# Input loads in thirds, and routed rows written one at a time over a longer stretch, in an attention-and-experts kernel

## The chip, the cores and the metric

The kernel runs on one core of a Trainium2 chip, as one program. The metric is the device time of one execution in microseconds; several executions are timed and their median counts. TensorE (PE in the rows, its weight loads PEld), VectorE (DVE), ScalarE (ACT), GpSimd (POOL) and SyncE (SP) each run their own instructions in program order, and wait for each other and for DMA transfers by semaphores. Plain transfers are issued on SP, indirect ones (rows addressed by a list of indices) on GpSimd.

## What is computed

Two steps in float32, cut from the reference. First a linear recurrence per batch (4) and head (8) over 768 steps with a head size of 48:

```python
for t in range(S):
    cur = einsum('bhd,bhe->bhde', u[None] * kt, vt)
    y[:, :, t] = einsum('bhd,bhde->bhe', rt, state + cur)
    state = wt[:, :, :, None] * state + einsum('bhd,bhe->bhde', kt, vt)
```

Then y, as 3072 rows x of 384, goes through a mixture of 8 experts with one expert per row:

```python
logits = x @ w_gate + modality_bias[modality_id]
e_idx = argmax(logits)
gate_w = probs[arange(N), e_idx]                 # softmax of logits
for e in range(E):
    h = maximum(x[e_idx == e] @ w1[e], 0.0)      # 384 -> 1024
    out[e_idx == e] = gate_w * (h @ w2[e])       # 1024 -> 384
```

## The kernel before

**Attention part.** The 3072 rows are cut into 24 units of 128 rows. The loop `for i in range(-2, NU)` calls `att_iter(i)`, which works on three units at a time: unit i+2 in its first stage (VectorE's scan and the spread of r and k), unit i+1 in its second (TensorE's scores, the mask A of L403, the state), unit i in its last (the products into pY, L445), while GpSimd prepares unit i+3 (the decays L278, G of L283, L295). The order of the work on each engine is the order in which the code is written; there is no scheduler.

A unit's inputs are r, k and w, each a third of 512 columns of one buffer `in0` to `in3` (768 KB for 128 partitions), and v, in a buffer of its own (4 of them). `load(n)` (L106) issues the transfer of unit n on SP, in one piece or cut by columns. SP works in order: a transfer whose buffer is still in use holds those behind it.

**Routing.** A unit's finished rows go into `xp` (L464), and once the rows of a part are routed (`route_a`, `route_b`), each unit's 128 rows of 386 columns are written to their places in the DRAM tile `xs` by one indirect transfer: `scatter(n)`, L692, on GpSimd, 128 row indices in a column of `posT`. `route_b` fills `posT` for all units of a part with one reduction (L574). Part 0 is units 0 to 9, part 1 units 10 to 23. `hook_b(c)` appends the units of part c to the list `pend`, and `drain(n)` scatters the next n of them. `pad_rows(e)` (L684, on SP) writes 128 rows of zeros behind expert e's rows. Rows of part 0 lie in memory that the weights of the first down-projection (`wh[1]`, `wl[1]`) use later.

**Experts part.** Seven blocks q0 to q6 of up to 512 routed rows. For each: `blk_load` reads the block's rows from `xs` into `xl` (L718, SP; block 0's and block 1's during attention, at the iterations in `LOAD`), `blk_t` transposes them (TensorE L733, ScalarE xh L743, VectorE xo L745), eight `blk_up` (the ups: 9 matmuls each, L756, into PSUM tile pS0 or pS1 in turn; then hh on ScalarE L760 and the remainder hl on VectorE L761), up to four `blk_down` (the downs, one for each 128 rows: 24 matmuls, L777), each with `blk_out` (ot on ScalarE L800, an indirect write of 128 output rows on GpSimd, L801). The weights come by `blk_raw` (L267, SP) and are split into a rounded part wh (ScalarE, L272) and a remainder wl (L273, GpSimd or VectorE) by `w_split`. A table, `at(q, "u" or "d", step, ...)`, says what else is written after each up ("u", steps 0 to 7) or after each two of a down's eight slices ("d", four steps for each down); `run` carries it out. By it the 14 units of part 1 are scattered two at a time after q0's "d" steps 2 to 8.

Transfers that read rows of `xs` wait for the scatters that were written ahead of them in the program to land, and scatters behind such a read wait until it has landed; scatters and pads are declared independent of each other.

Of the kernel before, what the change touches and what calls it, by code (L numbers as in the profile page):

```python
# [14 lines left out]
ALU = mybir.AluOpType  # L15
# [47 lines left out]
NEAR = 6  # L63
DRAIN = {**{SCATTER + 2 + n: 1 for n in range(NEAR)}, NU - 3: PART[0] - NEAR}
EARLY = 6
NPW = 3
LOAD = (SCATTER + 1 + NEAR, NU - 2)


@with_exitstack  # L70
def kernel(ctx: ExitStack, tc: tile.TileContext, rkw, vt, wf, cst, mid, wg, bias, w1, w2, out):
# [238 lines left out]
    def ok(n):  # L310
        return 0 <= n < NU
# [244 lines left out]
    def route_b(c):  # L556
# [13 lines left out]
        for j in range(n):  # L570
            m = n + (c == 0 and j < NEAR)
            add(pR[:, (j + 1) * E:(m + 1) * E], onesb, oh[:, j:j + 1].to_broadcast([P, m - j, E]), stop=j == n - 1)
        po, rk = posT[:, units(c)], rcol(C_RK, n, E)
        nc.vector.tensor_reduce(out=po, in_=rk, axis=AX.X, op=ALU.min)  # L574
        sm = wt(c, "sm", [P, NMOST, 1], 1)[:, 0:n]
        nc.vector.tensor_reduce(out=sm, in_=ex[:, 0:n], axis=AX.X, op=ALU.add)
        nc.vector.reciprocal(out=T["xp", c][:, :, DM:DM + 1], in_=sm)

    MAGIC = 12582912.0
# [143 lines left out]
    def blk_t(q):  # L723
        xl, w = X["xl", q], width(q)
        xh, xo = (bp["m"].tile([P, KC, BW], F32R, tag=t, name=f"{t}{q}", bufs=1) for t in ("xh", "xo"))
        pk, pu, nj = pt(f"x{q}_0", "pK", (P, 2, 512)), pt(f"x{q}_2", "pU"), w // P
        halves, m = [(0, KC - 1, (pk[:, 0], pk[:, 1])), (KC - 1, KC, (pu, pt(f"x{q}_3", "pX")))], w % P
        for c0, c1, pp in halves:
# [129 lines left out]
    def drain(n):  # L858
        for _ in range(n):
            if pend:  # L860
                scatter(pend.pop(0))

# [4 lines left out]
    for i in range(-2, NU):  # L867
# [13 lines left out]
        if i >= -1 and ok(i + 3):  # L881
            loadv(i + 3)
        if ok(i + 5):
            load(i + 5)
        if i == 0:
            early()

        drain(DRAIN.get(i, 0))
# [42 lines left out]
    at(q0, "d", 0, part(route_x, 1))  # L931
    at(q0, "d", 1, part(hook_b, 1))
    for g in range(2, 4 * FC // 2):
        at(q0, "d", g, part(drain, 2))
        if g < 6:
            at(q0, "d", g, part(w_split, 0, g - 2))
        if 5 <= g < 8:
            at(q0, "d", g, part(more_table, 1, 2 - g // 7))
# [5 lines left out]
    for e in range(E):  # L944
        at(q1, "u", e // 2, part(pad_rows, e))
    at(q1, "u", 4, part(blk_raw, seq[2], 0), part(blk_load, seq[2]))
    for k, q in enumerate(seq[1:1 + NG // 2]):
# [13 lines left out]
    for n, q in enumerate(seq):  # L961
# [5 lines left out]
        for g in range(FC):  # L967
            blk_up(q, g)
            run(q, "u", g)
        if nxt is not None:  # L970
            blk_t(nxt)
        for j in range(nj):
            for g in range(FC // 2):
                blk_down(q, (2 * g, 2 * g + 1), (j,))
# [199 lines left out]
```

## Time and profile before

| | us |
|---|---|
| timed runs | 362.39, 364.48, 364.92 |
| median of the three | 364.48 |
| profiled execution | 362.38 |
| span of its trace | 360.6 |
| TensorE busy | 338.0 (94%) |
| VectorE busy | 224.4 (62%) |
| ScalarE busy | 206.2 (57%) |
| GpSimd busy | 155.1 (43%) |
| mean granted TensorE clock | 0.972 of full |

The profiled execution took 362.38 us, of which 360.6 lie in the span. A busy share is an average over both parts, so the table alone says little: it is read by stretches (windows), in which one engine's busy time stands beside the clock that TensorE was granted (1.00 is its upper level, 2.4 GHz, and 0.50 its lower, 1.2 GHz) and the share of the time in which the DMA engines moved data. In a timeline each line is one instruction, or several alike in a row (x and their count): its start in the span, its duration, and in brackets how long the engine had been idle and what ended that. "issue" means that the profile shows nothing that the engine waited for, "remote" that what it waited for is not among the recorded events.

### The profile page before, as it was taken

How to read it: one execution, taken by the hardware profiler on the slowest of the kernel's cores; microseconds unless marked ns; L12 is line 12 of the kernel's file. 1: busy time of each engine (PE TensorE's matmuls, PEld its weight loads, DVE VectorE, ACT ScalarE, POOL GpSimd, SP SyncE). 2: the span in 40 equal slices, each digit the busy share in tenths (PEclk: the TensorE clock that was granted, in tenths of full speed). 3: DMA queues.
4: the chain of work that ended last, by engine and by line, in shares of the span. 5: the costliest groups of instructions: out<-in, count | busy, mean ns of one | idle time of the engine just before them, and what ended most of it. 6: DMA issues, size and time to landing. Idle time of an engine off the chain costs nothing.

```text
span 360.6 us, 10329 instructions
## 1 busy us (share of the span) xinstructions
PE 338.0 (94%) x4064; PEld 306.5 (85%) x4064; DVE 224.4 (62%) x478; ACT 206.2 (57%) x524; POOL 155.1 (43%) x194
## 2 busy tenths in 40 slices
PE   8899999999989799997499999999999999999993
PEld 3688899989889687896278999999999988999973
DVE  6999999999997244880057936946526525814500
ACT  2576687878789373620046835956956934614320
POOL 5889999999982860077410220120120120121013
PEclk9999999999999789999589999999999999999998
DMA  7977887778864320036640430160260442210001
GB/s 229 399 242 227 287 291 267 248 258 259 284 225 135 97 82 0 3 139 249 217 164 3 148 137 2 29 236 0 51 236 2 153 158 89 88 58 29 1 25 56
DMA packets 18910, 52.30 MB, mean 145 GB/s; under 512 B 2405, under 2 KB 10405, under 8 KB 18852
## 3 DMA queue, kind: packets, MB, share of 16 engines
q1 hardware_dynamic: 15748, 42.08, 35.3%
q0 software_dynamic: 3104, 9.47, 7.0%
q8 instruction: 34, 0.56, 0.7%
q14 instruction: 24, 0.20, 0.2%
HBM read 55.43 MB, written 11.88 MB: 187 GB/s over the span
## 4 chain that ended last, share of the span: by engine, by line
issue 52%; PE 11%; POOL 9%; POOLq 2%; DMA 1%; ACT 0%; DVE 0%; ACTq 0%
POOL out L801 6%; PE pY L445 3%; POOL xs L692 2%; PE pS L401 2%; PE pY L434 1%; POOLq L984 1%; PE pR_x L317 1%; PE pR_x L494 1%; PE pU L419 1%; DMA xs<-xp,posT 1%; PE pS_u L756 1%; POOL wl L273 1%; POOLq L801 0%; POOLq L964 0%; POOL xp L549 0%
## 5 line engine op out<-in xcount | busy, mean ns | idle before, releaser
L801 POOL DMA_INDIRECT out<-ot,xl x25 | 26.0, 1039 | 157.8 <-ACT ot L800 156.6
L761 DVE SCALAR_TENSOR_TENSOR hl<-pS_u,hh 128x512 fp32r<-128x512 f32 (+2 forms) x56 | 34.6, 618 | 88.3 <-ACT hh L760 74.8
L756 PE MATMUL pS_u<-xh,wh 128*128 128x512 f32 (+2 forms) x168 | 63.1, 375 | 3.0 <-issue 3.0
L756 PE MATMUL pS_u<-xh,wl 128*128 128x512 f32 (+2 forms) x168 | 62.4, 371 | 2.4 <-issue 2.4
L760 ACT ACTIVATE hh<-pS_u 128x512 fp32r<-128x512 f32 (+2 forms) x56 | 30.3, 541 | 51.7 <-PE pS_u L756 50.3
L273 DVE TENSOR_TENSOR wl<-raw,wh 128x768 fp32r<-128x768 f32 x52 | 48.2, 954 | 3.1 <-ACT wh L272 2.6
L756 PE MATMUL pS_u<-xo,wh 128*128 128x512 f32 (+2 forms) x168 | 44.2, 369 | 1.7 <-issue 1.7
L272 ACT CAST wh<-raw 128x768 fp32r<-128x768 f32 (+1 forms) x60 | 45.1, 800 | 0.0
L756 PEld LDWEIGHTS pS_u<-xh,wh 128*128 128x128 f32 x168 | 32.1, 191 | 9.0 <-issue 5.9
L692 POOL DMA_INDIRECT xs<-xp,posT x24 | 24.9, 1040 | 32.3 <-issue 25.0
L777 PE MATMUL pY_d<-wh,hh 128*128 128x384 f32 x112 | 38.5, 344 | 0.0
L777 PE MATMUL pY_d<-wl,hh 128*128 128x384 f32 x112 | 37.6, 336 | 0.0
L777 PE MATMUL pY_d<-wh,hl 128*128 128x384 f32 x112 | 37.6, 336 | 0.0
L756 PEld LDWEIGHTS pS_u<-xh,wl 128*128 128x128 f32 x168 | 32.1, 191 | 5.8 <-issue 2.8
L756 PEld LDWEIGHTS pS_u<-xo,wh 128*128 128x128 f32 x168 | 31.3, 190 | 5.0 <-issue 1.6
L331 DVE TENSOR_TENSOR_SCAN pX_s<-pw,pX_s 128x268 f32<-128x268 f32 x48 | 34.1, 710 | 1.1 <-POOL pw L278 0.8
L283 POOL TENSOR_TENSOR G<-in 128x512 f32<-128x512 f32 x24 | 31.0, 1293 | 4.6 <-DMA in<-rkw 4.6
L445 PE MATMUL pY<-v,A 128*64 128x48 f32 x768 | 29.0, 225 | 2.9 <-issue 2.9
L342 ACT ACTIVATE dV<-v,dT 128x48 f32<-128x48 f32 x120 | 29.7, 325 | 0.1
L445 PEld LDWEIGHTS pY<-v,A 128*64 128x64 f32 x768 | 26.3, 141 | 4.0 <-issue 3.7
L403 DVE TENSOR_TENSOR A<-pS,cs 128x1024 f32<-128x1024 f32 x24 | 29.2, 1217 | 0.6 <-PE pS L401 0.6
L401 PE MATMUL pS<-R,K 64*128 64x128 f32 x384 | 26.9, 280 | 2.0 <-DVE A L403 1.2
(327 smaller groups left out, 679.9 us busy)
## 6 DMA issues: line engine op xcount, KB each, us to landing
raw<-w SPq DMA_DIRECT2D x24, 768.0 KB
in<-rkw SPq DMA_DIRECT2D x22, 768.0 KB
v<-vt SPq DMA_DIRECT2D x24, 192.0 KB
wg<-wf SPq DMA_DIRECT2D x8, 576.0 KB
raw<-w SPq DMA_DIRECT2D x8, 384.0 KB
xl<-xs SPq DMA_DIRECT2D x3, 772.0 KB
xl<-xs SPq DMA_DIRECT2D x4, 579.0 KB
xs<-zt SPq DMA_DIRECT2D x8, 193.0 KB
```

Of the source, the lines that this page charges most:

```text
L272: nc.scalar.copy(out=wh[k][:, sl], in_=raw[k][:, sl])
L273: (eng or (nc.vector, nc.gpsimd)[k]).tensor_tensor(out=wl[k][:, sl], in0=raw[k][:, sl], in1=wh[k][:, sl].bitcast(F32), op=ALU.subtract)
L283: nc.gpsimd.tensor_tensor(out=G, in0=t[:, 0:512], in1=t[:, 512:1024], op=ALU.mult)
L331: nc.vector.tensor_tensor_scan(out=BE[:, ::step], data0=pp[:, ::step], data1=d1[:, ::step], initial=0.0, op0=ALU.mult, op1=ALU.max)
L401: nc.tensor.matmul(out=pS[:, hh, p], lhsT=K[q, p], rhs=R[q, p], start=True, stop=True)
L445: nc.tensor.matmul(out=pY[q:q + 64, h * D:(h + 1) * D], lhsT=A[:, hh, p, q:q + 64], rhs=v[:, h * D:(h + 1) * D], start=(first(z) and h == ...
L692: rows_apart("xs", nc.gpsimd.indirect_dma_start(out=xs[:, :], out_offset=bass.IndirectOffsetOnAxis(ap=posT[:, n:n + 1], axis=0), in_=T["xb ...
L756: nc.tensor.matmul(out=pp, lhsT=wsrc[0][:, g, c * P:(c + 1) * P], rhs=xsrc[:, c, 0:w], start=(n == 0), stop=(n == 3 * KC - 1))
L760: nc.scalar.activation(out=hh, in_=pp, func=AF.Relu)
L761: nc.vector.scalar_tensor_tensor(out=hl, in0=pp, scalar=0.0, in1=hh.bitcast(F32), op0=ALU.max, op1=ALU.subtract)
L777: nc.tensor.matmul(out=X["y", q, j][0:r1 - r0], lhsT=hsrc[:, r0:r1], rhs=wsrc[1][:, f], start=(f == 0 and n == 0), stop=(f == FC - 1 and n ...
L801: ins = nc.gpsimd.indirect_dma_start(out=out[:, :], out_offset=bass.IndirectOffsetOnAxis(ap=xl[0:m, j, DM + 1:DM + 2].bitcast(I32), axis=0 ...
```

## The change

Four things change; the computation stays the same.

1. **Loads.** Before, iteration i ended with unit i+5's whole load. Now unit 3 is loaded whole at i = -2, and from then on iteration i loads k and r of unit i+6, and w of unit i+6 (up to i = 0) and of unit i+7 (from i = 0 on), each as a transfer of 256 KB into its third of the buffer.
2. **Part-0 scatters.** Before, units 0 to 5 went out one at each iteration 15 to 20 and units 6 to 9 together at 21. Now units 0 to 7 go out one at each of 15 to 22 and units 8 and 9 at 23. Block 0's rows are still read at iteration 20, block 1's at 23 instead of 22.
3. **Part-1 scatters.** Before, two after each of seven "d" steps of block 0. Now one each after its "d" steps 2, 3, 4, 8 and 12, one after each of block 1's eight ups, and one after block 1's "d" step 0. Each is preceded by a reduction of its own unit's column of `posT` (`place`); part 0's is done at once as before.
4. **Block 2's rows.** They are read after block 1's "d" step 1 instead of after its up 4, and transposed ahead of block 1's last down instead of ahead of its first, with another PSUM tile.

```diff
--- before.py
+++ after.py
@@ -61,10 +61,10 @@
 NEARLY = 3
 SCATTER = PART[0] + 3
 NEAR = 6
-DRAIN = {**{SCATTER + 2 + n: 1 for n in range(NEAR)}, NU - 3: PART[0] - NEAR}
+DRAIN = {**{SCATTER + 2 + n: 1 for n in range(PART[0] - 2)}, NU - 1: 2}
 EARLY = 6
 NPW = 3
-LOAD = (SCATTER + 1 + NEAR, NU - 2)
+LOAD = (SCATTER + 1 + NEAR, NU - 1)
 
 
 @with_exitstack
@@ -570,11 +570,15 @@
         for j in range(n):
             m = n + (c == 0 and j < NEAR)
             add(pR[:, (j + 1) * E:(m + 1) * E], onesb, oh[:, j:j + 1].to_broadcast([P, m - j, E]), stop=j == n - 1)
-        po, rk = posT[:, units(c)], rcol(C_RK, n, E)
-        nc.vector.tensor_reduce(out=po, in_=rk, axis=AX.X, op=ALU.min)
+        if c == 0:
+            place(0, n)
         sm = wt(c, "sm", [P, NMOST, 1], 1)[:, 0:n]
         nc.vector.tensor_reduce(out=sm, in_=ex[:, 0:n], axis=AX.X, op=ALU.add)
         nc.vector.reciprocal(out=T["xp", c][:, :, DM:DM + 1], in_=sm)
+
+    def place(n, k):
+        c = int(n >= PART[0])
+        nc.vector.tensor_reduce(out=posT[:, n:n + k], in_=rcol(C_RK + (n - FROM[c]) * E, k, E), axis=AX.X, op=ALU.min)
 
     MAGIC = 12582912.0
 
@@ -724,7 +728,7 @@
         xl, w = X["xl", q], width(q)
         xh, xo = (bp["m"].tile([P, KC, BW], F32R, tag=t, name=f"{t}{q}", bufs=1) for t in ("xh", "xo"))
         pk, pu, nj = pt(f"x{q}_0", "pK", (P, 2, 512)), pt(f"x{q}_2", "pU"), w // P
-        halves, m = [(0, KC - 1, (pk[:, 0], pk[:, 1])), (KC - 1, KC, (pu, pt(f"x{q}_3", "pX")))], w % P
+        halves, m = [(0, KC - 1, (pk[:, 0], pk[:, 1])), (KC - 1, KC, (pu, pt(f"x{q}_3", "pS1" if q == WB else "pX")))], w % P
         for c0, c1, pp in halves:
             for c in range(c0, c1):
                 for j in range(nj):
@@ -858,7 +862,10 @@
     def drain(n):
         for _ in range(n):
             if pend:
-                scatter(pend.pop(0))
+                n = pend.pop(0)
+                if n >= PART[0]:
+                    place(n, 1)
+                scatter(n)
 
     def hook_b(c):
         route_b(c)
@@ -880,11 +887,18 @@
         att_iter(i)
         if i >= -1 and ok(i + 3):
             loadv(i + 3)
-        if ok(i + 5):
-            load(i + 5)
+        if i == -2:
+            load(3)
         if i == 0:
             early()
-
+        if ok(i + 6):
+            load(i + 6, ((512, 1024),))
+            load(i + 6, ((0, 512),))
+        for n in range(NEARLY):
+            if i == n - 2:
+                load(n + NIN, ((1024, LIN),))
+        if i >= NEARLY - 3 and ok(i + 3 + NIN):
+            load(i + 3 + NIN, ((1024, LIN),))
         drain(DRAIN.get(i, 0))
         if i in LOAD:
             blk_load(LOAD.index(i))
@@ -930,8 +944,10 @@
     at(q0, "u", FC - 1, part(next, ra1), part(next, ra1), part(blk_raw, q1, 1))
     at(q0, "d", 0, part(route_x, 1))
     at(q0, "d", 1, part(hook_b, 1))
+    for q, ph, steps in ((q0, "d", (2, 3, 4, 8, 12)), (q1, "u", range(FC)), (q1, "d", (0,))):
+        for g in steps:
+            at(q, ph, g, part(drain, 1))
     for g in range(2, 4 * FC // 2):
-        at(q0, "d", g, part(drain, 2))
         if g < 6:
             at(q0, "d", g, part(w_split, 0, g - 2))
         if 5 <= g < 8:
@@ -943,7 +959,8 @@
             at(q, "u", FC - 1, part(blk_raw, nq, 1))
     for e in range(E):
         at(q1, "u", e // 2, part(pad_rows, e))
-    at(q1, "u", 4, part(blk_raw, seq[2], 0), part(blk_load, seq[2]))
+    at(q1, "u", 4, part(blk_raw, seq[2], 0))
+    at(q1, "d", 1, part(blk_load, seq[2]))
     for k, q in enumerate(seq[1:1 + NG // 2]):
         for n, ph, step in ((2 * k, "u", 2), (2 * k + 1, "u", 6)):
             at(q, ph, step, part(guard_load, n))
@@ -967,9 +984,11 @@
         for g in range(FC):
             blk_up(q, g)
             run(q, "u", g)
-        if nxt is not None:
+        if nxt is not None and q != q1:
             blk_t(nxt)
         for j in range(nj):
+            if q == q1 and j == nj - 1:
+                blk_t(nxt)
             for g in range(FC // 2):
                 blk_down(q, (2 * g, 2 * g + 1), (j,))
                 if nxt is not None and q != q0 and j == 0:
```

GpSimd's rows at the end of the attention part and in blocks 0 and 1, before. `xp` are the routed rows (the first five scatter rows from the top are part 0's last five units, then part 1's fourteen), `dV` belongs to the attention part, `wl` are the remainders of block 0's first weights, `out<-ot` the output writes of block 0 (four) and block 1:

```order
L692 DMA xs<-xp_385,posT 29184x386
L354 TENSOR_TENSOR dV_2540<-v_2298,dT_2469 128x192
L692 DMA xs<-xp_385,posT 29184x386 x4
L354 TENSOR_TENSOR dV_2652<-v_2411,dT_2589 128x192
L273 TENSOR_TENSOR wl_69<-raw_66,wh_68 128x384 x3
L354 TENSOR_TENSOR dV_2738<-v_2524,dT_2683 128x192
L273 TENSOR_TENSOR wl_69<-raw_66,wh_68 128x384 x5
L549 COPY xp_1423<-tidi 128x14
L692 DMA xs<-xp_1423,posT 29184x386 x4
L801 DMA out<-ot_0_3128,xl_2529 3072x384
L692 DMA xs<-xp_1423,posT 29184x386 x8
L801 DMA out<-ot_1_3216,xl_2529 3072x384
```

The same place after the change:

```order
L696 DMA xs<-xp_393,posT 29184x386
L354 TENSOR_TENSOR dV_2580<-v_2339,dT_2509 128x192
L696 DMA xs<-xp_393,posT 29184x386
L354 TENSOR_TENSOR dV_2683<-v_2451,dT_2629 128x192
L273 TENSOR_TENSOR wl_69<-raw_66,wh_68 128x384 x3
L696 DMA xs<-xp_393,posT 29184x386
L354 TENSOR_TENSOR dV_2761<-v_2564,dT_2714 128x192
L273 TENSOR_TENSOR wl_69<-raw_66,wh_68 128x384 x5
L696 DMA xs<-xp_393,posT 29184x386 x2
L549 COPY xp_1451<-tidi 128x14
L696 DMA xs<-xp_1451,posT 29184x386 x2
L805 DMA out<-ot_0_3163,xl_2569 3072x384
```

```order
L696 DMA xs<-xp_1451,posT 29184x386
L805 DMA out<-ot_1_3231,xl_2569 3072x384
L696 DMA xs<-xp_1451,posT 29184x386
L805 DMA out<-ot_2_3265,xl_2569 3072x384
L696 DMA xs<-xp_1451,posT 29184x386
L805 DMA out<-ot_3_3299,xl_2569 3072x384
L696 DMA xs<-xp_1451,posT 29184x386 x9
```

Of part 0's last four units only one still stands ahead of the second-last `dV`; one stands ahead of the last `dV`, and two behind the five `wl`. In blocks 0 and 1 the four outputs of block 0 now stand between single scatters, and nine scatters follow the fourth output.

ScalarE's rows at the first ups of block 0, after the change, with their waits; `wh_2904` is the first cast into `wh[1]`, `hh` the activations of ups 0 and 1. The DMASW semaphores count the indirect transfers of GpSimd: the values waited for are those of all ten units of part 0, before and after the change alike.

```order
L272 CAST wh_68<-raw_66 128x384 x5
L764 ACTIVATE hh_0_2920<-pS_u_0_2910 128x512 [waits DMAHW3_49,DMAHW2_49,DMAHW7_49,PE_49,Activation_49]
L481 COPY xT_2926<-pX_('x', 0)_2925 128x384 [waits PE_49]
L272 CAST wh_2904<-raw_67 128x768 [waits DMASW4_49,DMASW3_49,DMASW5_49,DMASW2_49,DMASW6_49,DMASW1_49,DMASW7_49,DMASW0_49,DMAHW7_49,Activation_49,Pool_49]
L764 ACTIVATE hh_1_2943<-pS_u_1_2933 128x512 [waits PE_49]
```

The cast's place on ScalarE has not moved, but the last two scatters that it waits for now stand later on GpSimd.

SP's rows around the read of block 2's rows (`xl` of 3 x 128 rows; `raw_66` and `raw_67` are the weights w1 and w2 of block 2, `wg` a load for the guard), before and then after:

```order
L267 DMA raw_66<-w 128x1536
L717 TENSOR_LOAD tab
L717 ISA x2
L718 ISA
L718 DMA xl_3465<-xs 128x3x386
L452 DMA wg_3506<-wf 128x1152
L267 REGISTER_ALU x2
L267 ISA
L267 DMA raw_67<-w 128x1536
```

```order
L452 DMA wg_3540<-wf 128x1152
L267 REGISTER_ALU x2
L267 ISA
L267 DMA raw_67<-w 128x1536
L267 ISA
L267 REGISTER_ALU
L267 ISA
L267 DMA raw_67<-w 128x1536
L721 TENSOR_LOAD tab
L721 ISA x2
L722 ISA
L722 DMA xl_3584<-xs 128x3x386
```

The read of block 2's rows stood between the loads of block 2's two weights and now stands behind both.

## Rows read from the trace of the kernel before

**Rows 1.** Windows: us, busy time and count of each engine, granted clock, DMA share, GB/s:

```profile
core 0: us, PE busy (x) PEld busy (x) DVE busy (x) ACT busy (x) POOL busy (x), PEclk, DMA share, GB/s
...
27.00:108.00 81.00, 77.12 (x2004) 72.86 (x2002) 77.77 (x153) 62.67 (x228) 77.79 (x99) 1.00 0.79 261
...
117.00:126.00 9.00, 6.78 (x126) 5.77 (x122) 2.23 (x3) 3.58 (x12) 7.47 (x9) 0.77 0.30 96
126.00:135.00 9.00, 9.00 (x93) 7.83 (x90) 4.16 (x8) 6.90 (x18) 6.08 (x7) 0.85 0.24 85
...
150.00:166.00 16.00, 16.00 (x107) 15.84 (x106) 10.69 (x41) 5.09 (x10) 9.33 (x9) 1.00 0.39 138
...
171.00:181.00 10.00, 4.81 (x10) 2.46 (x9) 0.42 (x1) 1.52 (x3) 5.33 (x6) 0.60 0.64 217
...
184.00:355.00 171.00, 170.90 (x1006) 160.72 (x1004) 88.19 (x194) 95.09 (x164) 21.06 (x20) 1.00 0.25 85
```

**Rows 2.** Timeline of TensorE, 166 to 180: start, duration, what, idle before and releaser:

```profile
166.73 0.39 PE L756 MATMUL pS_u<-xh,wh 128*128 128x512 f32 x1
...
169.31 0.47 PE L756 MATMUL pS_u<-xo,wh 128*128 128x512 f32 x1 [0.79 <-issue]
...
179.22 0.58 PE L756 MATMUL pS_u<-xh,wl 128*128 128x512 f32 x1 [0.60 <-issue]
```

**Rows 3.** Timeline of ScalarE, 158 to 190:

```profile
158.61 0.58 ACT L800 ACTIVATE ot<-pX_d,xl 128x384 f32<-128x384 f32 x1 [2.12 <-PE pX_d L777]
169.29 0.58 ACT L800 ACTIVATE ot<-pY_d,xl 128x384 f32<-128x384 f32 x1 [10.10 <-remote]
179.47 0.58 ACT L800 ACTIVATE ot<-pX_d,xl 128x384 f32<-128x384 f32 x1 [9.60 <-remote]
...
186.72 0.60 ACT L760 ACTIVATE hh<-pS_u 128x512 fp32r<-128x512 f32 x1 [0.78 <-PE pS_u L756]
188.82 0.60 ACT L760 ACTIVATE hh<-pS_u 128x512 fp32r<-128x512 f32 x1 [1.50 <-PE pS_u L756]
```

**Rows 4.** Timeline of GpSimd, first and last of 17 indirect writes in a row:

```profile
154.23 1.79 POOL L692 DMA_INDIRECT xs<-xp,posT  x1 [19.54 <-issue]
...
175.89 0.98 POOL L801 DMA_INDIRECT out<-ot,xl  x1 [0.30 <-issue]
```

**Rows 5.** Timeline of TensorE in the attention part, behind a single scatter:

```profile
97.12 0.37 PE L445 MATMUL pY<-v,A 128*64 128x48 f32 x5 [0.69 <-issue]
```

**Rows 6.** Timeline of GpSimd, 117 to 134:

```profile
117.59 1.00 POOL L692 DMA_INDIRECT xs<-xp,posT  x1 [6.98 <-DMA xl<-xs]
...
121.45 0.97 POOL L692 DMA_INDIRECT xs<-xp,posT  x1 [0.31 <-issue]
...
128.88 4.91 POOL L273 TENSOR_TENSOR wl<-raw,wh 128x384 fp32r<-128x384 f32 x5 [2.60 <-ACT wh L272]
```

**Rows 7.** Timeline of ScalarE, 128 to 134:

```profile
128.29 2.17 ACT L272 CAST wh<-raw 128x384 fp32r<-128x384 f32 x5
...
132.74 0.85 ACT L272 CAST wh<-raw 128x768 fp32r<-128x768 f32 x1
```

**Rows 8.** Timeline of VectorE, 133 to 136:

```profile
133.62 1.00 DVE L273 TENSOR_TENSOR wl<-raw,wh 128x768 fp32r<-128x768 f32 x1
134.90 0.69 DVE L761 SCALAR_TENSOR_TENSOR hl<-pS_u,hh 128x512 fp32r<-128x512 f32 x1 [0.28 <-ACT hh L760]
```

**Rows 9.** Timeline of TensorE, first matmul of block 0's up 3:

```profile
137.03 0.51 PE L756 MATMUL pS_u<-xh,wh 128*128 128x512 f32 x1
```

**Rows 10.** SP's DMA issues: start, us to the last one's end, line, count:

```profile
111.98 12.88 SPq L718 DMA_DIRECT2D xl<-xs  x2
...
183.08 0.39 SPq L718 DMA_DIRECT2D xl<-xs  x1
```

**Rows 11.** DMA engines, 27 to 108: packets and bytes, loads of r, k, w:

```profile
DMA packets 6773, 21.14 MB, mean 261 GB/s; under 512 B 753, under 2 KB 3441, under 8 KB 6753
...
in<-rkw SPq DMA_DIRECT2D x16, 768.0 KB
```

## The prediction

> **What bounds the kernel now.** I read the table of windows first, because the kernel is two programs one after the other. In the attention part (27 to 108 us) TensorE, VectorE and GpSimd are each busy for 77 to 78 of 81 us and the DMA engines for 0.79 of the time [rows 1]: nothing there is far from being the bound, and no engine waits for long. From 184 to 355 us TensorE alone is the bound: 170.90 busy of 171.00 [rows 1]. So over the second part every microsecond that TensorE loses is a microsecond of the result, and the windows show two places where it loses some. From 117 to 126 it is busy 6.78 of 9 at a mean granted clock of 0.77, and from 171 to 181 only 4.81 of 10 at 0.60 [rows 1]. The 0.85 of 126 to 135 belongs to the first [rows 1].
>
> The second place is the large one. It lies in the eight ups of block 1 (L756). The timeline of TensorE shows the first up starting at 166.73; from 169.31 to 179.22 one matmul starts per 1.42 us (eight starts, seven intervals), and the releaser is "issue": the profile knows nothing that it waits for [rows 2]. ScalarE tells the same story from another side: the block's third and fourth outputs (L800) start at 169.29 and 179.47 after waits of 10.10 and 9.60 us put down to "remote", although TensorE had left the last down by 166.73; the second, at 158.61, had come promptly [rows 2, 3]. The first activation (L760) of block 1 stands behind the fourth output. Undisturbed ups follow each other by 188.82 - 186.72 = 2.10 us; four of them from 166.73 would have ended at 175.1, and the fourth's activation starts at 186.72, so about **11.4 us** are lost, idle time and low clock together [rows 2, 3].
>
> What lies in that stretch and not elsewhere is a burst on GpSimd: 17 indirect writes (14 scatters of L692, three outputs of L801) follow each other from 154.23 to 175.89 with 0.30 us between them [rows 4]. TensorE runs full through the first ten or so (150 to 166: 16.00 of 16) and then falls; about 3 us after the last it is back. The eight pad writes on SP (L684) are in the same stretch too, so the burst is the likely cause, not a proven one.
>
> **The change, part by part.** The sum is made against the profiled execution, 362.38 us. The three timed runs have their median at 364.48, 2.1 above it; for the median I add 1 us to the sum at its end.
>
> *Part-1 scatters apart.* Instead of 14 scatters in a row, five fall in the downs of block 0, eight in the ups of block 1 (one per up) and one in its downs, with the outputs between them. If the burst is the cause, the 11.4 us come back. What do single scatters cost? No row shows one beside an up. The lower bound is nothing: 20 single outputs, the same kind of instruction, lie in 184 to 355, where TensorE loses 0.10 us in all [rows 1]. The upper bound is the attention part, where gaps of TensorE put down to "issue" stand a microsecond or two behind single scatters, the longest of them 0.69 us [rows 5]: eight of them are 5.5 us. The ups are nearer to the first case (large matmuls, two PSUM buffers, 2.10 us against 0.60 + 0.69 for activation and remainder [rows 3, 8]), so I take 0.25 each, **2.0 us** (0 to 5.5).
>
> *Part-0 scatters later.* The first place is 117 to 126. GpSimd's seventh scatter waits 6.98 us for block 0's rows to be read, then four scatters go out to 121.45, and TensorE's gaps fall into them [rows 6]. Up to 2.22 us of idle time, and by the clocks 0.23 x 6.78 + 0.15 x 9 = 2.9 us of slow running, hang on that: 5.1 us [rows 1]. But the scatters moved away don't vanish. The 7.0 us wait stays, since the seventh scatter still stands behind that read. Scatters 8 and 9 (counting from 0) now stand behind the five wl of the next stretch on GpSimd. ScalarE's first cast into wh[1] (132.74 now [rows 7]), whose memory held the rows of part 0, waits until all ten have landed. Before, that was long past. After: the five wl start at 128.88 now, 0.6 after ScalarE's five casts at 128.29, and those follow TensorE's transposes; taking the whole 2.2 us of gaps away, the wl start at 126.7 and end 4.91 later at 131.6 [rows 6, 7]. Scatter 8 starts at 131.6, scatter 9 at 132.9. The last landing of the old four shows the time of flight: from 121.45 to SP's issue that waits for it, which ends at 111.98 + 12.88 = 124.86, less 0.39 for the issue itself, is 3.0 us [rows 6, 10]. So the cast runs at 135.9 to 136.75. VectorE's wl (1.00) and the remainder of up 1 (0.69) stand behind it: 138.4 [rows 7, 8]. Up 3 needs up 1's PSUM buffer; it started at 137.03 [rows 9]. The gain of the first place is eaten and up 3 comes **1.4 us later**. Ends: if the casts come 2.5 us sooner than I reckon, -1; if the clock falls in the idle time of about 4.5 us ahead of up 3, and stays low as long after, half of 4.5 more, +3.7.
>
> *Block 1's rows.* Their load now goes out behind scatter 9's landing, at about 136 instead of 124.5. A load of 772 KB takes at most 117.59 - 111.98 = 5.6 us [rows 6, 10], so 141.6; they are transposed after eight ups, past 148. Nothing lost.
>
> *Block 2's rows.* Call the end of block 1's ups T0. The remainder of up 7 (0.69), a wl (1.00), the small reduction and the last scatter put its start at about T0 + 3; 3.0 of flight, 0.4 of issue and 5.6 of load give T0 + 12.0, or T0 + 10.6 if 579 KB take their share of the 5.6. Its transposes now stand ahead of the last down, after three of about 4.1 us (two lie between 158.5 and 166.73 [rows 2, 3]): T0 + 12.3. It fits, with 0.3 to 1.7 us to spare: **0**, and each microsecond later costs one.
>
> *The reductions.* Fourteen of one column, each below the 0.69 us of a 512-column remainder [rows 8], on a VectorE that has more than half of each up free: 0 (0 to 1).
>
> *Loads in thirds.* Each third goes out when its own third is free, one unit earlier for k and r, and at most two for w. With the DMA engines at 0.79 and one load per 5 us there is room [rows 1, 11]: the 16 loads of 768 KB become 48 of 256 KB, and three issues of 0.4 us for each unit fit on SP. I take 0, with +-1. The Trainium skill speaks against it ("DMA: Bandwidth & Descriptors", section "Rules for kernel authors"): transfers of at least 1 MiB for the best rate, small ones joined. That is rival 5; no row here shows a load of 256 KB.
>
> The sum: 362.4 - 11.4 + 2.0 + 1.4 = 354.4, and 355.5 for the median.
>
> **The rivals.**
> 1. *Both places gain.* ScalarE's cast isn't held, because the wl are done earlier or the landing is quicker: 362.4 - 9.4 - 5.1 = 347.9. Against it: two scatters of 1.28 us and a flight of 3.0 behind 4.91 us of wl are in the order. Chance 0.09.
> 2. *The burst is not the cause*, and the change doesn't do what it says: the slow issue belongs to the pads, or to writes in flight of any spacing. The pads stay in block 1's ups and go out earlier. From no gain, 363.8, to half of it, 358.1. For it: TensorE ran full through the first half of the burst [rows 1]. Chance 0.20, half of it within 1%.
> 3. *Slower: each scatter holds the ups for its flight.* If signals are late while any scatter is in flight, each of nine costs 3.0 less the slack of an up (2.10 - 0.60 - 0.69 = 0.8): 2.2, and 19.8 in all, against 11.4 before: 362.4 - 11.4 + 19.8 + 1.4 = 372.2. It breaks even at (11.4 - 1.4)/9 = 1.1 us per scatter. Against it: the 20 single outputs without a loss, and 0.69 as the longest gap behind a single scatter. Chance 0.08.
> 4. *Block 2's rows come late*, by 2 to 4 us, because of pads or weights in the queues: 356 to 358. Chance 0.08.
> 5. *Loads in thirds slow the attention part.* The loads are 16 x 0.786 = 12.6 of 21.14 MB there [rows 11]. If a third's bytes took m times as long, the DMA share would be 0.79 x (0.4 + 0.6 m): full at m = 1.44; at 1.6 it is 1.07, which costs 0.07 x 81 = 6 us: 360. Chance 0.05.
>
> **How the numbers follow.** My forecast, with its own range 351 to 358.5 (terms 2.0 and 1.4 at their ends), has 0.50. A measurement of this kernel can tell about 1%, 3.6 us, from no change. Faster by more: forecast, rivals 1 and 4, half of 2 and part of 5, 0.77. Within 1%: the rest of 2 and 5, 0.15. Slower: rival 3, 0.08. The range from 348 to 364 leaves out half of rival 1 and rival 3, and some tail.
>
> **What would show it.** Right: from 166 to the end of block 1's ups TensorE advances by 2.1 to 2.4 us per up, no "remote" wait of L800 above 2 us, and the clock stays at its upper level; a wait of ScalarE at the wh[1] cast of 3 us or more that ends on the scatters, with up 3 near 138. Wrong: "issue" gaps of TensorE that follow the scatters into the ups (rivals 2, 3), a wait of TensorE's transposes on block 2's rows (4), GpSimd's G (L283) waiting for loads (5), or a cast without a wait (1).

## The result and the profile after

The changed kernel takes 353.06 us (median of six, 351.44 to 354.38) against 363.79 us (median of six, 362.39 to 366.73) for the kernel before beside it: a ratio of 0.9712, 95% interval 0.9675 to 0.9749. The profiled execution took 352.71 us, its span is 350.9 instead of 360.6. The forecast was 355.5, between 348 and 364. Some single executions, of several kernels, ran a part of the attention at TensorE's lower clock: the comparisons leave out the slowest of them, and of the profiled ones with a granted clock under 1.00 between 27 and 108 us (e2, e3, e4, e7 and e9) mainly blocks 0 and 1 are read.

The windows of the changed kernel, over the stretches of [rows 1]:

```profile
core 0: us, PE busy (x) PEld busy (x) DVE busy (x) ACT busy (x) POOL busy (x), PEclk, DMA share, GB/s
27.00:108.00 81.00, 79.14 (x2044) 74.90 (x2042) 78.17 (x152) 64.38 (x234) 78.71 (x99) 1.00 0.81 257
...
117.00:126.00 9.00, 9.00 (x155) 7.97 (x154) 3.67 (x7) 7.78 (x23) 7.60 (x9) 1.00 0.11 38
126.00:135.00 9.00, 3.36 (x26) 2.52 (x25) 1.87 (x3) 2.73 (x5) 3.90 (x5) 0.92 0.32 98
135.00:150.00 15.00, 15.00 (x57) 11.37 (x57) 6.20 (x11) 4.09 (x8) 0.00 (x0) 0.71 0.06 21
...
171.00:181.00 10.00, 10.00 (x44) 8.07 (x43) 6.12 (x13) 4.88 (x8) 5.14 (x5) 1.00 0.78 244
```

and one more window of the kernel before:

```profile
135.00:150.00 15.00, 15.00 (x105) 11.70 (x104) 8.55 (x14) 6.94 (x13) 0.00 (x0) 1.00 0.01 2
```

171 to 181 is now full, 10.00 of 10 at a clock of 1.00, where it was 4.81 at 0.60 [rows 1]. 117 to 126, the prediction's first place, is full too, 9.00 of 9 at 1.00 where it was 6.78 at 0.77 [rows 1]. In exchange 126 to 135 holds 3.36 of 9 and 135 to 150 has a clock of 0.71: before, TensorE was busy for 9.00 in the first [rows 1], and the clock of the second was 1.00. Two stalls have gone and another has come, so the places are read by themselves.

**Block 0's ups.** ScalarE and TensorE in the changed kernel:

```profile
123.88 0.60 ACT L764 ACTIVATE hh<-pS_u 128x512 fp32r<-128x512 f32 x1
...
132.27 0.83 ACT L272 CAST wh<-raw 128x768 fp32r<-128x768 f32 x1 [7.42 <-issue]
133.01 0.59 ACT L764 ACTIVATE hh<-pS_u 128x512 fp32r<-128x512 f32 x1
```

```profile
126.31 0.48 PE L760 MATMUL pS_u<-xh,wh 128*128 128x512 f32 x1
...
134.75 0.80 PE L760 MATMUL pS_u<-xh,wh 128*128 128x512 f32 x1 [5.64 <-DVE hl L765]
...
139.63 0.80 PE L760 MATMUL pS_u<-xh,wh 128*128 128x512 f32 x1
...
143.64 0.45 PE L760 MATMUL pS_u<-xh,wh 128*128 128x512 f32 x1
```

ScalarE does the activation of up 0 at 123.88 and then holds the first cast into `wh[1]` until 132.27; up 1's activation follows at 133.01, and TensorE, which had started up 2 at 126.31, waits 5.64 us for up 1's remainder. GpSimd shows why:

```profile
115.24 1.01 POOL L696 DMA_INDIRECT xs<-xp,posT  x1 [6.51 <-DMA xl<-xs]
...
122.81 4.88 POOL L273 TENSOR_TENSOR wl<-raw,wh 128x384 fp32r<-128x384 f32 x5
127.87 1.01 POOL L696 DMA_INDIRECT xs<-xp,posT  x1 [0.17 <-issue]
129.18 0.98 POOL L696 DMA_INDIRECT xs<-xp,posT  x1 [0.30 <-issue]
```

The five wl end at 127.7, the last two scatters of part 0 start at 127.87 and 129.18, and 3.1 us after the last of them, its flight, the cast starts. Then the price that the prediction kept as an end of its range falls due: up 3 takes from 134.75 to 139.63 and up 4 to 143.64, 4.9 and 4.0 us instead of 2.75 and 2.20, because the clock has fallen in the idle time. (A single matmul shows it: 0.80 us at 134.75 against 0.45 at 143.64.) Scatter 6 still waits for the read of block 0's rows, at 115.24 (117.59 in [rows 6]).

**Block 1's ups.** ScalarE and GpSimd:

```profile
164.48 0.58 ACT L804 ACTIVATE ot<-pY_d,xl 128x384 f32<-128x384 f32 x1 [3.58 <-PE pY_d L781]
168.64 0.58 ACT L804 ACTIVATE ot<-pX_d,xl 128x384 f32<-128x384 f32 x1 [3.58 <-PE pX_d L781]
...
172.83 0.60 ACT L764 ACTIVATE hh<-pS_u 128x512 fp32r<-128x512 f32 x1 [0.78 <-PE pS_u L760]
174.93 0.60 ACT L764 ACTIVATE hh<-pS_u 128x512 fp32r<-128x512 f32 x1 [1.50 <-issue]
```

```profile
172.40 1.49 POOL L696 DMA_INDIRECT xs<-xp,posT  x1 [1.93 <-DVE posT L581]
174.50 0.98 POOL L696 DMA_INDIRECT xs<-xp,posT  x1 [0.61 <-DVE posT L581]
...
188.96 1.50 POOL L696 DMA_INDIRECT xs<-xp,posT  x1 [0.31 <-DVE wl L273]
```

The third and fourth outputs come promptly, at 164.48 and 168.64, and the ups run at 2.10 us each (172.83 to 174.93) with one scatter beside each. They took 28.3 us before (166.73 to 195.0) and take 16.8 now.

The account from stage to stage goes by what TensorE does next after each block's ups. After block 0's, in both kernels, it transposes block 1's rows; after block 1's, it transposes block 2's rows in the kernel before and starts block 1's first down in the changed one. The kernel before, then the changed one:

```profile
148.37 0.71 PE L733 MATMUL pK_x<-cs,xl 64*128 64x64 f32 x16
...
195.01 0.59 PE L733 MATMUL pK_x<-cs,xl 64*128 64x64 f32 x12
```

```profile
150.09 0.71 PE L737 MATMUL pK_x<-cs,xl 64*128 64x64 f32 x16
...
185.24 0.33 PE L781 MATMUL pY_d<-wh,hh 128*128 128x384 f32 x1
```

Block 0's ups end at 150.1 instead of 148.4 (1.7 later), block 1's at 185.2 instead of 195.0 (9.8 earlier, so 11.5 gained in between), and that difference stays to the end: 350.9 against 360.6.

### The profile page after: what moved, and what is told of

The parts are those of the page before. It is cut to its first block, busy times and chain, and to the rows that moved or that the text cites. A ratio compares the mean times of both kernels' runs of the same rounds, so it can differ in the third digit from the quotient of the medians.

```text
span 350.9 us, 10452 instructions
## 1 busy us (share of the span) xinstructions
PE 333.8 (95%) x4064; PEld 305.8 (87%) x4064; DVE 224.8 (64%) x491; ACT 206.0 (59%) x524; POOL 156.1 (44%) x194
## 4 chain that ended last, share of the span: by engine, by line
issue 41%; PE 28%; POOL 7%; ACT 3%; POOLq 2%; DVE 1%; ACTq 0%; DVEq 0%
PE pS_u L760 9%; POOL out L805 5%; PE pY L445 3%; PE pS L401 3%; PE pY_d L781 2%; PE pX_d L781 2%; PE pY L434 2%; PE pR_x L317 2%; PE pU L419 2%; POOLq L1003 1%; PE pR_x L494 1%; POOL wl L273 1%; ACT dV L342 1%; POOL xs L696 1%; ACT pU L422 1%
## 5 line engine op out<-in xcount | busy, mean ns | idle before, releaser
L696 POOL DMA_INDIRECT xs<-xp,posT x24 | 27.1, 1129 | 44.6 <-DVE posT L581 35.5
L781 PE MATMUL pY_d<-wh,hh 128*128 128x384 f32 x112 | 38.4, 343 | 0.0
L781 PE MATMUL pY_d<-wh,hl 128*128 128x384 f32 x112 | 37.6, 336 | 0.0
L781 PE MATMUL pY_d<-wl,hh 128*128 128x384 f32 x112 | 37.6, 336 | 0.0
L295 POOL TENSOR_TENSOR in<-in 128x512 f32<-128x512 f32 (+1 forms) x23 | 28.3, 1230 | 0.6
L445 PE MATMUL pY<-v,A 128*64 128x48 f32 x768 | 27.6, 222 | 0.4 <-issue 0.3
```

The costliest lines, as they stand in the source:

```text
L445: nc.tensor.matmul(out=pY[q:q + 64, h * D:(h + 1) * D], lhsT=A[:, hh, p, q:q + 64], rhs=v[:, h * D:(h + 1) * D], start=(first(z) and h == ...
L696: rows_apart("xs", nc.gpsimd.indirect_dma_start(out=xs[:, :], out_offset=bass.IndirectOffsetOnAxis(ap=posT[:, n:n + 1], axis=0), in_=T["xb ...
L781: nc.tensor.matmul(out=X["y", q, j][0:r1 - r0], lhsT=hsrc[:, r0:r1], rhs=wsrc[1][:, f], start=(f == 0 and n == 0), stop=(f == FC - 1 and n ...
```

## The experiments

The runs fell on four chips, and that turned out to matter as much as any edit: the kernel before takes 363.0 and 363.4 us on two of them (called chips 1 and 4 here), near the 363.79 of the result, whose chip is not recorded, and 348.0 to 349.1 us on the other two (chips 9 and 14). Chip 14 was used twice, a quarter of an hour apart, with chip 1 in between, and gave 349.1 and 348.8, so the difference goes with the chip and not with the hour; which core of a chip ran the kernel isn't recorded. Every ratio below is to the kernel before on the same chip. Two theories stood at the start. Theory 1: the row of 17 indirect writes on GpSimd slows the other engines and makes block 1's ups slow. Theory 2: the cast into `wh[1]` holds block 0's ups for the last two scatters of part 0.

**The burst back (e1, chip 9).**

```diff
-    for q, ph, steps in ((q0, "d", (2, 3, 4, 8, 12)), (q1, "u", range(FC)), (q1, "d", (0,))):
-        for g in steps:
-            at(q, ph, g, part(drain, 1))
     for g in range(2, 4 * FC // 2):
+        at(q0, "d", g, part(drain, 2))
```

> The changed kernel with the 14 scatters of part 1 put back two at a time after block 0's down steps 2 to 8 (each still with its own one-column reduction); loads, part 0 and the late read of block 2's rows stay as changed. Theory 1, the burst of indirect writes slows the ups of block 1: the slow issue of TensorE (about 1.4 us per matmul) and the waits of L804 put down to remote come back, block 1's ups take about 28 us again instead of 16.8, and the time is about 353 + 11 = 364 us. Rival, it was the earlier read of block 2's rows or the pads that slowed the ups: the time stays at 353 us, the ups at 16.8.

Measured: 351.11 us, ratio 1.0111 (1.0071 to 1.0150), beside a kernel before at 348.0. Its 18 writes stand in a row from 152.79 to 175.41, and TensorE is busy 17.00 of 17 us between 166 and 183: the ups take 2.1 us each. Theory 1 as written had failed, but so had the yardstick: 348 is not 364.

**The burst back, pads late (e2, chip 9).** As e1, with `at(q1, "d", 0, part(pad_rows, e))` in place of `at(q1, "u", e // 2, ...)`.

> As the kernel with the burst back, and the eight pad writes moved behind block 1's down step 0, so that SP issues none of them while the burst runs. If the burst of indirect writes is enough by itself: the ups still take about 28 us. If burst and pads together are needed: 17 to 20 us. Behind the ups the read of block 2's rows waits for the late pads, some 8 us of issuing, so TensorE will wait for them ahead of block 1's last down, 3 to 8 us, in both cases; the ups alone are compared.

Measured: 361.13 us, ratio 1.0379 (1.0266 to 1.0492). On this chip the ups were not slow with the pads either, so the question of burst or pads stays unanswered by it. What it does show is rival 4: SP issues the pads from 187.65 and block 2's read only after them, and TensorE waits 5.01 us ahead of block 1's last down. The wait is not the whole 10 us by which e2 lies above e1: there were only two executions, and the profiled one is later by 2.7 us already in the attention part (scatter 6 at 118.19 against 115.46) and runs at the lower clock behind the wait.

**Only part 1 spaced (e3, chip 9).** The changed kernel with the loads, `DRAIN` and `LOAD` of the kernel before.

> The changed kernel with the loads whole and part 0's scatters and block 1's read placed as before: only the part-1 scatters spaced and block 2's rows later. Theory: the 11.4 us of block 1's ups are gained in full and nothing is lost at the first ups of block 0: 362.4 - 11.4 = 351 us in the profile, 352.5 in the median, some 1.7 us less than with the whole change; no wait of ScalarE at the first cast into wh[1]. Rival, the three parts help each other: 356 us or more.

Measured: 349.54 us, ratio 1.0003 (0.9954 to 1.0051). Where the ups aren't slow, spacing the writes and reading block 2's rows later neither gains nor costs anything that can be measured.

**Both kernels again (e4 and e5, chip 14).** No edit.

> The kernel before, unaltered, on the chip of this job, since the runs beside the last experiments took 348 us and not 364. Theory 1 as it stood (the burst by itself slows the ups of block 1) expects 28 us for those eight ups wherever the kernel runs, and 362 to 366 us in all. Rival, that chip or its state sets whether the ups slow down: the burst is there, the ups take 16.8 us, and the time is near 348 us.

> The changed kernel, unaltered, beside it on the same chip. Theory 1: 351 to 354 us, 10 us faster than before here too. Rival: 351 to 354 us as well, since it has no slow ups to lose, but then 3 to 5 us slower than the kernel before on this chip, by the 5.6 us wait of TensorE in block 0's ups and the low clock behind it.

Measured: before 349.08 us, after 353.83, ratio 1.0213 (1.0109 to 1.0317): on this chip the change makes the kernel slower, by 1.1 to 3.2%. A window of the kernel before here, and its indirect writes:

```profile
171.00:181.00 10.00, 10.00 (x45) 8.04 (x44) 5.86 (x8) 4.64 (x8) 7.00 (x7) 1.00 0.70 228
```

```profile
155.09 1.79 POOL L692 DMA_INDIRECT xs<-xp,posT  x1 [18.44 <-issue]
...
178.84 0.98 POOL L801 DMA_INDIRECT out<-ot,xl  x1 [0.30 <-issue]
```

The same burst, 18 writes from 155.09 to 178.84 with 0.30 us between them, and TensorE at 10.00 of 10 us where [rows 1] has 4.81. So the rival of that expectation holds: the burst alone does not make the ups slow; something that goes with the chip decides. What the change costs is there on this chip too; TensorE in the changed kernel:

```profile
134.60 0.79 PE L760 MATMUL pS_u<-xh,wh 128*128 128x512 f32 x1 [5.34 <-DVE hl L765]
```

**Three at 22 (e6, chip 9).**

```diff
-DRAIN = {**{SCATTER + 2 + n: 1 for n in range(PART[0] - 2)}, NU - 1: 2}
+DRAIN = {**{SCATTER + 2 + n: 1 for n in range(PART[0] - 3)}, NU - 2: 3}
```

> The changed kernel with units 7, 8 and 9 scattered together at iteration 22 instead of 7 there and 8 and 9 at 23, so that all part-0 rows leave GpSimd ahead of the five wl. Theory 2, the cast into wh[1] holds the ups because two scatters stand behind the wl: the 7.4 us wait of ScalarE and the 5.6 us of TensorE shrink below 1.5 us, the clock stays at its upper level through block 0's ups, which end 8 to 9 us earlier: about 345 us. Rival, three scatters in a row make gaps of TensorE of the old size, 2 us and some us of low clock: 349 us. Rival, the wait at the cast is on something else: 353 us.

Measured: 347.52 us, ratio 0.9967 (0.9916 to 1.0018); e1, which has the wait of the changed kernel (5.47 us), took 351.11 on the same chip, and the single times of the two don't overlap (345.81 to 349.83, with 357.60 left out, against 350.08 to 353.07). e1 has the burst besides, which costs nothing there (e3). Theory 2 holds: with the scatters ahead of the wl TensorE's wait is 2.41 us instead of 5.5. It is not the 1.5 or less that I expected; TensorE and VectorE:

```profile
131.58 0.50 PE L760 MATMUL pS_u<-xh,wh 128*128 128x512 f32 x1 [2.41 <-DVE hl L765]
```

```profile
127.72 3.21 DVE L273 TENSOR_TENSOR wl<-raw,wh 128x768 fp32r<-128x768 f32 x1 [1.84 <-ACT wh L272]
130.85 1.27 DVE L765 SCALAR_TENSOR_TENSOR hl<-pS_u,hh 128x512 fp32r<-128x512 f32 x2
132.04 0.94 DVE L273 TENSOR_TENSOR wl<-raw,wh 128x768 fp32r<-128x768 f32 x1
```

VectorE's wl takes 3.21 us there and 0.94 four us later. It lies beside GpSimd's five wl, which run from 125.22 to 130.1. The remainder of up 1, which up 3 waits for, stands behind it. That GpSimd's wl hold up VectorE's is what the overlap suggests (e7 has the same 3.21 and 0.94); GpSimd's own five take 4.88 us, as in the changed kernel, where VectorE has no wl beside them. No run takes it apart.

**Two and two, spaced and as a burst; loads alone (e7, e8, e9, chip 1).** e7 is the changed kernel with part 0's last four units two at iteration 21 and two at 22 (`DRAIN = {**{SCATTER + 2 + n: 1 for n in range(NEAR)}, NU - 3: 2, NU - 2: 2}`); e8 is e7 with e1's edit; e9 is the kernel before with the loads of the change.

> The changed kernel with part 0's last four units scattered two at iteration 21 and two at 22, so that all are out ahead of the five wl and the last lands 1 us sooner than with three at 22. Theory 2 (the cast into wh[1] holds the ups): TensorE's wait in block 0's ups falls from 5.5 us to about 1 to 2.5 us, what is left of it being VectorE's wl beside GpSimd's; 345 to 347 us on any chip. On a chip where the kernel before takes 348 us that is 1 to 3 us less than before; on one where it takes 364 us, 17 to 19 less. Rival, the wait is not the scatters': 351 to 353 us.

> The same with part 1's scatters two at a time again, a burst of 17 indirect writes. Theory 1 holds only where the kernel before takes 364 us: there this one takes about 357 us, with 28 us of ups in block 1. Where the kernel before takes 348 us the burst costs nothing in the ups: the same time as the spaced one within 1 us, or 1 us less, since block 2's rows are ready sooner.

> The kernel before with the loads in thirds alone. The sum of the prediction took 0 (within 1 us) for them. Theory 3, formed since, from scatter 6 starting at 115.2 with thirds and at 117.6 to 122 with whole loads: units reach GpSimd sooner, and the attention part ends 2 to 4 us earlier: 345 to 346 us where before takes 348. Rival: those 2 to 4 us are the low clock of single runs, and the time is that of before.

Measured beside a kernel before at 362.95: e7 346.69 us, ratio 0.9522 (0.9447 to 0.9597); e8 358.99 us, 0.9889 (0.9808 to 0.9971); e9 361.50 us, 0.9962 (0.9923 to 1.0002). Here chip and edit are separated. In e7 the wait in block 0's ups is nearly gone, and the clock stays at 1.00 through them:

```profile
134.34 0.50 PE L760 MATMUL pS_u<-xh,wh 128*128 128x512 f32 x1 [1.14 <-DVE hl L765]
```

e7 and e8 differ in nothing but the places of part 1's scatters (and with them the outputs between), and the burst costs 12.3 us. GpSimd, TensorE, ScalarE and the windows of e8:

```profile
148.33 1.05 POOL L696 DMA_INDIRECT xs<-xp,posT  x1 [17.64 <-DVE posT L581]
...
167.66 0.98 POOL L696 DMA_INDIRECT xs<-xp,posT  x1 [0.30 <-issue]
```

```profile
161.99 0.48 PE L781 MATMUL pX_d<-wh,hl 128*128 128x384 f32 x1 [1.71 <-issue]
...
168.29 0.48 PE L781 MATMUL pX_d<-wh,hl 128*128 128x384 f32 x1 [1.62 <-issue]
...
171.11 0.67 PE L781 MATMUL pX_d<-wl,hh 128*128 128x384 f32 x1 [0.25 <-issue]
```

```profile
171.24 0.58 ACT L804 ACTIVATE ot<-pY_d,xl 128x384 f32<-128x384 f32 x1 [17.80 <-remote]
```

```profile
160.00:171.00 11.00, 2.67 (x6) 1.35 (x6) 0.00 (x0) 0.00 (x0) 6.81 (x7) 0.59 0.48 180
```

Two things differ from [rows 2 to 4]. The slow stretch lies in block 0's downs (L781) this time, because the burst starts 6 us earlier: it is not the ups that are slow but whatever TensorE does from some 12 us after the first of 16 writes (the first gap begins at 160.3) until about 3 us after the last (167.66). And the steps are 2.1 us for one matmul, not 1.42. ScalarE's third output waits 17.80 us, again for nothing that is recorded, and VectorE is idle from 160 to 171. ScalarE is late before TensorE is: that third output belongs to a down whose last matmul ended at 157.0. In e9, with the burst and of the change only the loads, TensorE is busy 4.60 of 10 us from 171 to 181, as before:

```profile
171.00:181.00 10.00, 4.60 (x9) 2.19 (x9) 0.00 (x0) 0.51 (x2) 5.33 (x6) 0.63 0.65 224
```

So on a chip of this kind the burst brings the slow stretch about, and spacing it takes the stretch away. The early read of block 2's rows isn't needed for it, since e8 reads them as late as the changed kernel does; the pads stood beside the burst in every run that had the stretch. The loads alone are the same within the interval, 1.5 us at the medians.

**Narrow writes (e10, chip 14).** e7 with 14 more indirect writes ahead of part 1's, of 16 columns each into scratch tiles.

> The spaced kernel with two and two (346.7 us), with 14 further indirect writes of 128 rows of 16 columns each (64 bytes a row instead of 1544) into scratch tiles, two at a time after block 0's down steps 2 to 8, so that GpSimd again issues some 20 indirect writes back to back but moves a third of the bytes. On a chip where the kernel before takes 363 us: if the rate of issue on GpSimd is what slows the other engines, TensorE stalls as with the wide burst, about 357 to 360 us; if it is the bytes written, 347 to 349 us. On a chip where before takes 348 us: 347 to 349 us either way, and nothing is told apart.

Measured: 352.0 us, ratio 1.0128 (1.0036 to 1.0219). The chip was one without slow stretches, so bytes and rate of issue are not told apart. The loss is rival 4 once more: the real scatters come later, and TensorE waits 4.78 us for block 2's rows:

```profile
194.12 0.91 PE L738 MATMUL pK_x<-cs,xl 64*128 64x64 f32 x12 [4.78 <-DMA xl<-xs]
```

**Two rows of seven (e11, chip 14; e12, chip 4).** e7 with seven scatters at once after block 0's down step 2 and seven after block 1's up 2.

```diff
-    for q, ph, steps in ((q0, "d", (2, 3, 4, 8, 12)), (q1, "u", range(FC)), (q1, "d", (0,))):
-        for g in steps:
-            at(q, ph, g, part(drain, 1))
+    for q, ph, step in ((q0, "d", 2), (q1, "u", 2)):
+        at(q, ph, step, part(drain, 7))
```

> The kernel with two and two, with part 1's 14 scatters in two rows of seven, after block 0's down step 2 and after block 1's up 2, some 9 us of pause or single outputs between them. On a chip where the kernel before takes 363 us the slow stretches began 12 to 14 us after the first write of a row of 17, so if they need that many in a row, seven (9 us) make none: 347 us. If each write adds its share, about 0.7 us, the sum stays near 10 us: 356 us. On a chip where before takes 348 us: 347 us.

> The two rows of seven once more, for a chip on which the kernel before takes 363 us (the first time it fell on one where before takes 348.8 and this one 345.3). There: 347 us if a row of seven is too short to slow the other engines, as theory 1 with its 12 us of delay has it; 356 us if each write of a row adds its share. On a chip where before takes 348: 345 us, with TensorE's wait in block 0's ups at 1.2 us.

Measured: e11 345.31 us, ratio 0.9927 (0.9883 to 0.9972), beside 348.83; e12 346.52 us, ratio 0.9573 (0.9492 to 0.9655), beside 363.40. GpSimd and the windows of e12:

```profile
149.46 1.42 POOL L696 DMA_INDIRECT xs<-xp,posT  x1 [17.63 <-DVE posT L581]
...
161.92 0.98 POOL L805 DMA_INDIRECT out<-ot,xl  x1 [0.30 <-issue]
165.40 0.98 POOL L805 DMA_INDIRECT out<-ot,xl  x1 [2.50 <-ACT ot L804]
170.47 0.98 POOL L696 DMA_INDIRECT xs<-xp,posT  x1 [4.09 <-DVE posT L581]
...
178.19 0.98 POOL L696 DMA_INDIRECT xs<-xp,posT  x1 [0.30 <-issue]
```

```profile
150.00:166.00 16.00, 16.00 (x88) 15.28 (x87) 6.90 (x30) 4.49 (x8) 10.75 (x11) 1.00 0.63 220
166.00:171.00 5.00, 5.00 (x23) 3.78 (x22) 3.47 (x12) 2.37 (x5) 0.91 (x2) 1.00 0.61 196
171.00:181.00 10.00, 10.00 (x47) 8.40 (x46) 5.49 (x8) 4.13 (x7) 6.34 (x7) 1.00 0.48 184
```

Ten writes in a row (149.46 to 161.92, three outputs behind the seven) and later seven more leave TensorE at 16.00 of 16, 5.00 of 5 and 10.00 of 10. As many scatters as in e8, on a chip on which the kernel before is slow too, and no slow stretch of TensorE. So it is not that each write takes its share of TensorE's time: as far as chip 4 is of the kind of chip 1 (the long row was tried there only as the kernel before), it takes a longer row than ten. The row of ten does leave a trace on ScalarE:

```profile
159.99 0.58 ACT L804 ACTIVATE ot<-pY_d,xl 128x384 f32<-128x384 f32 x1 [5.41 <-PE pX_d L781]
164.55 0.58 ACT L804 ACTIVATE ot<-pX_d,xl 128x384 f32<-128x384 f32 x1 [3.98 <-PE pS_u L760]
```

Block 0's third and fourth downs ended at 158.1 and 162.3, so these outputs are 1.9 and 2.3 us late; in e7, and in e11 on chip 14, they follow within 0.1 us. This speaks for chip 4 being of the kind of chip 1, and it suggests, without showing it, that a row of ten begins what a longer one carries on to TensorE. With e7 this kernel is the best measured: 346.52 and 346.69, not to be told apart, some 1.9% below the changed kernel where that was recorded (353.06, though not on the same chip). It is faster than the kernel before on both kinds of chip, on chip 14 by 0.3 to 1.2%.

## Why the prediction was right

**Part-1 scatters apart: right, and the residue was too high.** The 11.4 us came back, 11.5 by the account. The 2.0 us that I kept for eight single scatters were 0: the ups take 2.10 us each with a scatter beside every one. The range allowed for 0 to 5.5. The row that I thought nearer, the single outputs without a loss in 184 to 355 [rows 1], was the right one; the gap of 0.69 [rows 5], among small matmuls, did not carry over.

**The new wait: right in place and cause, and close in size by luck, because two errors cancel.** The cast waited for scatters 8 and 9 behind the five wl, as the code's order told. I had the wl end at 131.6 and the cast at 135.9; they ended at 127.7 and it ran at 132.27, some 3.6 us sooner, of which 2.35 stand already in the attention part (scatter 6 at 115.24 instead of 117.59). Against that the clock fell and ups 3 and 4 took 8.9 us instead of some 5.0. These 3.9 us are of this execution: after waits of 5.47 and 5.34 us the same two ups took 6.3 in e1 and 7.0 in e5. The end of the ups came 1.7 us later, where the sum had 1.4 and its end 3.7. What the sum didn't say is what the first place was worth: without that wait the kernel gains some 6.4 us more (346.69 in e7 against 353.06, though not on the same chip; on one chip e6 gains 3.6 on e1, with 2.41 us of wait left).

**Loads in thirds: 0 was within what can be told.** e9 has 0.9962 (0.9923 to 1.0002). Rival 5 cost nothing here: 256 KB transfers carried 257 GB/s at a DMA share of 0.81 in the window from 27 to 108, beside 261 at 0.79 with 768 KB [rows 1], and all four compute engines are a little busier there than before. By the prediction's own formula the share rose as for m = 1.07 (an estimate from these two rows: 0.81/257 against 0.79/261 is 1.04 for all the bytes), far from the 1.44 at which it would be full. The Trainium skill ("DMA: Bandwidth & Descriptors", section "Rules for kernel authors") asks for at least 1 MiB per transfer for the best rate, and for joining many small ones into a large one. No run here shows time lost by going the other way (e9). Whether the 2.35 us by which the attention part was ahead are the loads' isn't settled: among the executions with thirds scatter 6 started at 115.0 to 115.8 in e1, e5, e6, e8, e10, e11 and e12 and, with some of the attention at the lower clock, at 116.45 in e7; of those with whole loads only the 117.59 of the kernel before can be set beside them.

**Block 2's rows: right, and tight.** The last scatter started at 188.96 (T0 + 3.8, I had T0 + 3), SP's issue ended by 193.3, and the transposes ran at 197.81 without a wait, so the load took at most 4.5 us, near the lower of the two values that the prediction allowed (4.2 and 5.6):

```profile
192.93 0.40 SPq L722 DMA_DIRECT2D xl<-xs  x1
```

```profile
197.81 0.59 PE L737 MATMUL pK_x<-cs,xl 64*128 64x64 f32 x12
```

In e2 and e10, where the read came later, TensorE waited 5.01 and 4.78 us at that place, as rival 4 describes.

**Rival 2, the burst not the cause: half true.** On chips 1 and 4 the length of the row of writes decides (e7, e8, e12). On chips 9 and 14 it doesn't matter, since no stall is there to lose. The prediction read one profile of one chip and took the 11.4 us for a property of the kernel. The recorded gain of 2.9% is that of a chip with the stall; on chip 14 the same change costs 2.1%. That sign was in no rival of mine: what makes it slower there is not rival 3's flight of each scatter but the same wait on the cast that is a term of the sum, without the 11.4 us to pay for it. That the recorded comparison fell on a chip with the stall was luck. The trace of before did carry a hint that I named and went past: "issue" on TensorE and "remote" on ScalarE at the same time, with no dependence of the program that would explain either.

**The range.** The prediction's own range, 351 to 358.5, is said to be that of its terms 2.0 and 1.4 at their ends; the lower end is (350.0, and 351.0 for the median), but with 5.5 and 3.7 the upper one would be 360.2, and 361.2 for the median. The measured 353.06 is inside either.

**Open.** What differs between the chips, and where the other 4 of the 15 us between them lie; whether the bytes, the descriptors or the pace of issue on GpSimd bring the slow stretch about; and whether the pads on SP have to be there (e2 and e10 fell on chips that could not show it). Pads without a long row make none: that is e7 on chip 1.

## What to carry to other kernels

When instructions are moved to make room, list what waits for the last of them: two scatters moved behind five weight splits held a cast, and after the idle time of 5.6 us the low clock cost 3.9 more (1.3 and 2.1 in e1 and e5). A stall that the profile puts down to no dependence should be looked for on a second chip before it is taken as the kernel's own, and a change that removes it should be judged by what else it adds. Indirect writes need not be spread evenly: here rows of seven with a pause were as good as single ones, and the last scatter went out 6.4 us sooner (178.19 in e12, 184.57 in e7).

## What the runs showed of the hardware

- The same kernel took 348 to 349 us on two chips and 363 to 364 on others. Some 11 of the 15 us lie in one stretch, in which TensorE issues one matmul per 1.4 to 2.1 us, ScalarE starts on a finished down 12.7 us late (179.47 against 166.73 [rows 2, 3]), and SP takes 17.86 us for six pad writes in e8 (6.45 in e7 on the same chip).
- There TensorE's slow stretch began 12 us after the first of 16 indirect writes 1.28 us apart in e8 (14 us after the first of 17 in the kernel before) and ended about 3 us after the last. A row of ten made none on TensorE (e12), but two outputs on ScalarE came 1.9 and 2.3 us late.
- A VectorE tensor_tensor of 128x768 took 3.21 us beside GpSimd's wl (128x384 each), and 0.94 after them (e6 and e7).
- After 5.64 us in which TensorE waited, its clock was at the lower level from the first matmul on, for 8.9 us of full work in the changed kernel; after 5.47 us in e1 ups 3 and 4 took 6.3 us, and after 1.14 us in e7 the clock stayed at 1.00.
